# Twelve of 25 blocks of attention weights turned on VectorE and exchanged through DRAM instead of on TensorE

## The chip, the cores and the metric

The kernel runs on one core of a Trainium2 chip. The metric is the device time of one launch in microseconds (us).

## The reference

Attention over 8 batches, 8 heads, 576 positions and 64 channels with a block mask, then a two-layer feed-forward with ELU over 4608 tokens, then a soft mixture of 8 experts with 4 slots each:

```python
scores = scale * np.matmul(q, k.transpose(0, 1, 3, 2))
mask = block_i >= block_j                    # blocks of 64 positions
attn = np.exp(scores - max) / sum            # over the unmasked keys
attn_out = np.matmul(attn, v)
h = x @ w_in                                 # 4608x512 @ 512x2048
g = np.where(h > 0.0, h, np.exp(np.minimum(h, 0.0)) - 1.0)
x = g @ w_out                                # 4608x2048 @ 2048x512
logits = x @ phi                             # 512 x 32 slots
slot_input = softmax(logits, over tokens).T @ x
slot_out = relu(slot_input @ w1) @ w2        # per expert
out = softmax(logits, over slots) @ slot_out
```

All data is float32.

## The kernel before

The work is recorded as operations with an engine, a duration, the buffers read and written and a key (`Plan.add`), and `Plan.order` sets the order by a simulated list schedule: each engine takes, of the operations whose inputs are ready by the planner's durations, the one with the lowest key. On the chip each engine then runs its list in order and waits where an input is late. DMAs are all issued from SyncE's queue (SP), but for the first pair.

**Attention** goes by 32 pairs of heads (four pairs are one batch of 576 tokens). For a pair, `pair_load` and `pair_prep` bring q and k with the channels on partitions. `pair_scores` (four fills, lines 527 to 535) makes the scores on TensorE, takes row maxima on VectorE (L546) and exponentials with row sums on ScalarE (L549); the fourth fill holds the two units (1,0) and (1,1), 128 queries by 256 keys each. `pair_weights` then takes reciprocals (L561, L562), multiplies the weights on GpSimd (L566), and turns them so that the keys lie on partitions: 25 blocks of 128x128 per pair, each one TensorE matmul against the identity (L322), in groups of up to four that go to a PSUM bank and are copied to SBUF by ScalarE or VectorE (L298, L300). A unit (u, h) is 128 queries of head h with 128(u+1) keys, so it has u+1 blocks; the unit "b" holds the last 64 queries of both heads and has five. 8+6+4+2 blocks and those five make 25. `pair_values` multiplies them with v (L632, L636): per pair and head six accumulating pieces of 64, 512, 448, 320, 192 and 64 columns, with the two heads in the two halves of TensorE's columns. The result goes to a ring of two batches (`XR`). The first eight pairs load and scale q and k in another way (`NTP = 8`), and run partly ahead of the rest.

**The feed-forward** goes by 36 tiles of 128 tokens: per tile four ranges of 512 hidden units, per range four steps of three matmuls of 512 columns in fp32r (high and low parts, L669 to L671). Exponential on ScalarE (L674), minimum and maximum on VectorE (L676, L679). In tiles 0 to 29 the hidden units g are turned for the logits without TensorE: VectorE turns 32x32 blocks (`STREAM_TRANSPOSE`, L687), SP writes them to a DRAM tile `turned` (512 KB, twice per tile) and reads them back with the blocks exchanged over partitions (four reads of 128 KB, in runs of 1 KB). `tile_routing` (L711) and `tile_dispatch` (L733 to L771) follow; their 32-column matmuls use a quarter of TensorE's columns each.

**The tail** loads the experts' weights into 23 slots of 1 MB as they come free (among them the attention's SBUF area) and runs the expert layers and the output product.

In idle stretches of the start and of the tail TensorE runs small filler matmuls (L1037). A fp32 matmul shows twice in the trace (two passes) and once in the order of the built program; fp32r matmuls and the identity matmuls show once in both.

The change touches `Plan.add` and `Plan.order` (L77 and L100), `pair_load` (L433), `pair_scores` (L513), `pair_weights` (L552), `pair_values` (L622), the durations handed to the planner in the tile functions, the SBUF area of the turned weights (`PT`), and the key of each pair (`base` in the loop over pairs at the end):

```python
base = T * 4.5 * (b - 1) + 24.0 * p - 24.0 if b else KAS * p + KA0
```

Of the kernel before, what the change touches and what calls it, by code (L numbers as in the profile page):

```python
# [10 lines left out]
F32 = mybir.dt.float32  # L11
# [7 lines left out]
P = 128  # L19
# [5 lines left out]
RING = 2 * S  # L25
KWIN, KWOUT, KWP, KWPS = -92.0, -42.0, 2.0, 2.0
KWS, KWOS, KA0, KAS, KCON, KLD, KSTAGE, NPB = 3.5, 1.0, -109.0, 14.0, -150.0, 30.0, 26.0, 4
NEV, NQ = 16, 1
TLAG, LATE, NTP = 2.5, 30, 8
TICK, DUTY, FILL, FN = 3.4, 0.5, 0.055, 128  # L30
SCALE = 0.125
MASKED = -1e9
# [19 lines left out]
class Plan:  # L52
# [9 lines left out]
    def __init__(self):  # L62
        self.ops = []
        self.writers = {}
        self.readers = {}
        self.fills = []
        self.load = {}
        self.lag = {}

        self.slack = {}  # L70

    def fill(self, dur, fn, after, until):


        self.fills.append((dur, fn, after, until))

    def add(self, engs, dur, fn, r=(), w=(), key=0.0, nbytes=0, load=1.0, lag=1.0, slack=0.0):  # L77
        if isinstance(engs, str):
            engs = (engs,)
        if not isinstance(dur, tuple):  # L80
            dur = (dur,) * len(engs)
        i = len(self.ops)
        deps = set()
        for b in r:
            deps |= set(self.writers.get(b, ()))
        for b in w:
            deps |= set(self.readers.get(b, ()))
            deps |= set(self.writers.get(b, ()))
        for b in r:
            self.readers.setdefault(b, []).append(i)  # L90
        for b in w:
            self.writers[b] = [i]
            self.readers[b] = []
        self.ops.append((engs, dur, fn, deps, key, nbytes))
        self.load[i] = load
        self.lag[i] = lag
        self.slack[i] = slack
        return i

    def order(self):  # L100
        n = len(self.ops)
# [14 lines left out]
        finish = [1e9] * n  # L116
        recent = []
        fillers = {}

        def rested(now):  # L120

# [11 lines left out]
        while events:  # L133
            now = events[0][0]
            while events and events[0][0] <= now + 1e-9:
                _, kind, i = heapq.heappop(events)
                if kind == 0:
                    for e in self.ops[i][0]:
                        heapq.heappush(heaps[e], (self.ops[i][4], i))
            for e in engines:  # L140
                if free[e] > now + 1e-9:
                    continue
                h = heaps[e]
                while h and done[h[0][1]]:
                    heapq.heappop(h)
                if not h:
                    if e == "PE" and rested(now):
                        for d, fn, after, until in self.fills:
                            if finish[after] <= now and not done[until]:
                                seq.append((now, -1, e))  # L150
                                fillers[len(seq) - 1] = fn
                                free[e] = now + d
                                recent.append((now, now + d, 1.0))
                                heapq.heappush(events, (free[e], 1, -1))
                                break
                    continue
                _, i = heapq.heappop(h)
                done[i] = True
                engs, dur, fn, deps, key, nbytes = self.ops[i]
                d = dur[engs.index(e)]  # L160
                busy[e] += d
# [21 lines left out]
        self.span = max(free.values())  # L183
        self.busy = busy
        self.fillers = fillers
        return [(fillers[j] if i < 0 else self.ops[i][2], e) for j, (_, i, e) in enumerate(seq)]


# [16 lines left out]
def attention_moe_kernel(ctx: ExitStack, tc, q, k, v, w_in, w_out, phi, w1, w2, consts, out):  # L205
# [26 lines left out]
    PAD = TT  # L232
    NPT = 2
    PTW = 4 * CHS + S
    PT = aa.take(2 * NPT * PTW)
    RQ = aa.take(2 * S)
    RK = aa.take(2 * S)
    QT = aa.take(2 * S)
# [19 lines left out]
    as_u32 = [t.bitcast(U32) for t in tiles]  # L258
    ps = pp.tile([P, 4096], F32, name="ps")
    wo_f32 = dpool.tile([FF, DM], F32, name="wo_f32")  # L260
    turned = [dpool.tile([P, 1024], F32, name="turned%d" % j) for j in range(2)]
    successors = {}
    marks = {}
# [173 lines left out]
    def pair_load(n, key):  # L437
# [14 lines left out]
        for src, base, nm in ((q, RQ, "rq"), (k, RK, "rk")):  # L452
            for a in range(4):
                h, db = 2 * p + a // 2, a % 2
                load(f(base + S * s, S, 32 * a, 32 * a + 32).rearrange("p (t i) -> p t i", i=32),
                     src[b, h, :, 32 * db:32 * db + 32].rearrange("(t j) i -> j t i", j=32), 340000,
                     w=[(nm, s, a)], key=key, eng=queue(n))

    def pair_load_v(n, key):
# [51 lines left out]
    def pair_scores(n, fill, key):  # L511
# [11 lines left out]
        def sc(e):  # L523
# [15 lines left out]
        add("PE", (0.0 if last else 0.2) + cols / 600, sc, r=([("qb", s, 0), ("qb", s, 1)] if last else [("qt", s)]) + [("kt", s)], w=bkeys, key=key,  # L539
            load=1.0)  # L540
# [13 lines left out]
    def pair_weights(n, half, key):  # L554
# [9 lines left out]
        for x in units:  # L564
            p = pat(x, n)
            add("POOL", (0.28 + wide(x) / 1050) * (1.3 if n < 8 else 1.0), lambda e, x=x, p=p: nc.gpsimd.tensor_scalar(  # L566
                out=f(p, wide(x)), in0=f(p, wide(x)), scalar1=f(rs_col + 9 * s + UNITS[x][0], 1), scalar2=0.0,
                op0=ALU.mult, op1=ALU.add), r=[("rs", s, half)], w=[pkey(x, n)], key=key)

        sl = n % NPT  # L570
        pt = PT + 2 * PTW * sl
# [47 lines left out]

    pt_keys = {}  # L620

    def pair_values(n, key):  # L622
        b, p = divmod(n, 4)
        vs = V + 640 * (n % NV)
        sl = n % NPT
# [12 lines left out]
        add("PE", 2.9, pv, r=rd, w=["ptb", "pvb"], key=key, load=0.25)  # L638
# [22 lines left out]
    def tile_range(i, r, hb, gs, ts, kr):  # L661
# [4 lines left out]
        for kk in range(4):  # L666
# [6 lines left out]
            add("PE", 0.65, hm, r=[("xh", s), ("xl", s), ("wh", r, kk), ("wl", r, kk)], w=[("h", hb)], key=kr)  # L673
# [32 lines left out]
    def tile_routing(kp):  # L706
        def lg(e):
            for c in range(16):
                j = c % 4
                gt = f(GT + 1024 * (c // 8), 1024).rearrange("p (a c j) -> p c a j", a=4, j=32)[:, c % 8]  # L710
                mm(pb(POST, P, 32 * j, 32 * j + 32), lhsT=f(WP + NS * c, NS), rhs=gt, start=(c < 4), stop=(c >= 12))  # L711
        add("PE", 1.0, lg, r=["wp"] + gtk(0) + gtk(1), w=["post"], key=kp, load=0.25)

    def tile_logits(r, ts, bank, bk, kp):
        def lg(e):
            for j in range(4):
                mm(pb(bank, P, 32 * j, 32 * j + 32), lhsT=f(WP + NS * (4 * r + j), NS), rhs=f(ts[0] + P * j, P),
                   start=(r == 0), stop=(r == 3))
        add("PE", 0.3, lg, r=["wp"] + ts[1], w=[bk], key=kp, load=0.25)

    def tile_dispatch(tiles, gs, banks, lps, dtx, dx, kp):

# [46 lines left out]
        add("PE", 0.95 * n, disp, r=[dx[1]] + [gs[t][j][1] for t in range(n) for j in range(4)], w=[bk], key=kp, load=0.25)  # L769
# [35 lines left out]
    def tail(key):  # L805
        att = [(nm, s, a) for nm in ("rq", "rk") for s in range(2) for a in range(4)] + [(nm, s) for nm in ("qt", "kt") for s in range(2)] + \
              [("v", s, j) for s in range(NV) for j in range(3)] + [pkey(x, s) for x in UNITS for s in range(2)] + \
              [x for s in range(NPT) for x in pt_keys[s]]
# [205 lines left out]
    ev = []  # L1014
    for n in range(NPAIR):
        b, p = divmod(n, 4)
        base = T * 4.5 * (b - 1) + 24.0 * p - 24.0 if b else KAS * p + KA0
        ev.append((base - (27 if n < NTP else KLD), lambda n=n, x=base - KLD: pair_load(n, x)))
        ev.append((base - 14, lambda n=n, x=base - 14: pair_prep(n, x)))
        ev.append((base - 16, lambda n=n, x=base - 16: pair_load_v(n, x)))  # L1020
# [4 lines left out]
        ev.append((base + 24, lambda n=n, x=base + 24: pair_values(n, x)))  # L1025
# [46 lines left out]
```

## Time and profile before

| | us |
|---|---|
| three runs, median (lowest to highest) | 993.82 (993.13 to 994.99) |
| profiled execution, span from first to last instruction | 992.1 |
| TensorE busy | 957.2 |
| VectorE, ScalarE, GpSimd busy | 632.8, 474.1, 269.9 |

For the profiled execution the page gives the span; its time outside the span is not told apart, and the span lies 1.7 us below the median of the runs. Engine names in rows: PE is TensorE's matmuls and PEld its weight loads, DVE VectorE, ACT ScalarE, POOL GpSimd, SP SyncE; a q behind the name is the engine's sequencer, as in SPq. L669 is line 669 of the kernel before. Matmuls are pipelined: the duration of one includes its way through the array, so what a matmul costs on the path is read from the chain of waits, which counts each stretch of time once, and not from the mean duration of one.

### The profile page before, as it was taken

How to read it: one execution, taken by the hardware profiler on the slowest of the kernel's cores; microseconds unless marked ns; L12 is line 12 of the kernel's file. 1: busy time of each engine (PE TensorE's matmuls, PEld its weight loads, DVE VectorE, ACT ScalarE, POOL GpSimd, SP SyncE). 2: the span in 40 equal slices, each digit the busy share in tenths (PEclk: the TensorE clock that was granted, in tenths of full speed). 3: DMA queues.
4: the chain of work that ended last, by engine and by line, in shares of the span. 5: the costliest groups of instructions: out<-in, count | busy, mean ns of one | idle time of the engine just before them, and what ended most of it. 6: DMA issues, size and time to landing. Idle time of an engine off the chain costs nothing.

```text
span 992.1 us, 19100 instructions
## 1 busy us (share of the span) xinstructions
PE 957.2 (96%) x6829; PEld 654.1 (66%) x6829; DVE 632.8 (64%) x1612; ACT 474.1 (48%) x1322; POOL 269.9 (27%) x425
## 2 busy tenths in 40 slices
PE   8989999999999999999999999999999999999992
PEld 6657776676666766766666676666666677776351
DVE  5987876566556666667777776777767664444151
ACT  5865555454545555544445444454454343222143
POOL 3852432322212332322332223223232221000000
PEclk9999999999999999999999999999999999999996
DMA  9747567754445445645454445454533249149969
GB/s 239 216 129 214 173 198 177 156 138 127 110 130 142 123 115 126 153 113 141 121 133 123 130 122 137 126 144 115 127 108 101 83 138 401 56 138 326 351 231 354
DMA packets 243998, 160.86 MB, mean 162 GB/s; under 512 B 178624, under 2 KB 209472, under 8 KB 243904
## 3 DMA queue, kind: packets, MB, share of 16 engines
q1 hardware_dynamic: 242704, 159.35, 56.1%
q8 instruction: 54, 0.88, 0.4%
q10 hardware_dynamic: 1200, 0.30, 0.1%
q14 instruction: 40, 0.33, 0.1%
HBM read 114.51 MB, written 45.09 MB: 161 GB/s over the span
## 4 chain that ended last, share of the span: by engine, by line
PE 87%; DMA 4%; ACT 3%; DVE 3%; issue 1%; POOL 1%; SPq 1%; ACTq 0%; DVEq 0%; POOLq 0%
PE ps L669 15%; PE ps L671 13%; PE ps L670 13%; PE ps L322 12%; PE ps L636 8%; PE ps L535 8%; PE ps L767 4%; PE ps L711 3%; PE ps L527 2%; DMA att<-in_moe_w_dram 1%; PE ps L419 1%; DMA g<-in_moe_w_in_dram 1%; PE ps L938 1%; PE ps L1037 1%; ACT att L549 1%; PE ps L733 1%
## 5 line engine op out<-in xcount | busy, mean ns | idle before, releaser
L669 PE MATMUL ps<-w,xhl 128*128 128x512 f32 x576 | 253.3, 440 | 1.2 <-DVE g L679 1.2
L566 POOL TENSOR_SCALAR att<-att,base 128x128 f32<-128x128 f32 (+4 forms) x288 | 177.8, 636 | 206.7 <-DVE base L562 177.7
L671 PE MATMUL ps<-w,xhl 128*128 128x512 f32 x576 | 226.9, 394 | 0.0
L670 PE MATMUL ps<-w,xhl 128*128 128x512 f32 x576 | 226.1, 393 | 0.0
L549 ACT ACTIVATE att<-ps,base 128x128 f32<-128x128 f32 (+4 forms) x288 | 157.8, 553 | 97.1 <-DVE base L546 93.9
L298 ACT COPY att<-ps 128x512 f32<-128x512 f32 (+3 forms) x233 | 110.6, 511 | 92.7 <-PE ps L322 82.4
L546 DVE TENSOR_REDUCE base<-ps 128x1 f32<-128x128 f32 (+4 forms) x288 | 136.5, 502 | 24.4 <-ACT att L549 12.3
L674 ACT ACTIVATE xe<-ps 128x512 f32<-128x512 f32 x144 | 86.2, 599 | 134.7 <-PE ps L671 131.5
L676 DVE TENSOR_SCALAR xe<-xe 128x512 f32<-128x512 f32 x144 | 68.1, 473 | 121.4 <-ACT xe L674 120.9
L669 PEld LDWEIGHTS ps<-w,xhl 128*128 128x128 f32 x576 | 108.3, 188 | 54.7 <-issue 32.7
L322 PE MATMUL ps<-base,att 128*128 128x128 f32 (+1 forms) x880 | 131.1, 279 | 7.4 <-POOL att L566 5.6
L322 PEld LDWEIGHTS ps<-base,att 128*128 128x128 f32 (+1 forms) x880 | 101.4, 142 | 46.0 <-POOL att L566 15.7
L671 PEld LDWEIGHTS ps<-w,xhl 128*128 128x128 f32 x576 | 108.1, 188 | 25.0
L670 PEld LDWEIGHTS ps<-w,xhl 128*128 128x128 f32 x576 | 108.9, 189 | 13.5
L535 PE MATMUL ps<-att 64*128 64x128 f32 (+3 forms) x512 | 96.0, 468 | 3.7 <-ACT att L549 3.6
L679 DVE TENSOR_TENSOR g<-xe,ps 128x512 f32<-128x512 f32 x144 | 97.3, 677 | 2.2
L656 POOL TENSOR_TENSOR xhl<-xe,xhl 128x512 fp32r<-128x512 f32 x36 | 47.3, 1316 | 159.5 <-ACT xhl L654 144.8
L636 PE MATMUL ps<-att 128*64 128x512 f32 (+4 forms) x640 | 88.3, 422 | 0.0
L687 DVE STREAM_TRANSPOSE g<-g 128x512 f32<-128x512 f32 x120 | 82.6, 691 | 3.8 <-DMA turned<-g 1.6
L636 PEld LDWEIGHTS ps<-att 128*64 128x64 f32 x640 | 43.3, 137 | 42.4 <-issue 33.2
L535 PEld LDWEIGHTS ps<-att 64*128 64x128 f32 x512 | 42.0, 185 | 37.9 <-issue 15.7
L487 POOL TENSOR_SCALAR base<-att 64x64 f32<-64x64 f32 x48 | 11.8, 246 | 198.6 <-DVE att L484 141.9
(127 smaller groups left out, 1058.3 us busy)
## 6 DMA issues: line engine op xcount, KB each, us to landing
turned<-g SPq DMA_DIRECT2D x60, 512.0 KB, 3.1
g<-turned SPq DMA_DIRECT2D x240, 128.0 KB, 3.1
att<-in_moe_w_dram SPq DMA_DIRECT2D x11, 1024.0 KB, 13.7
att<-in_v_dram SPq DMA_DIRECT2D x64, 128.0 KB, 3.0
g<-in_moe_w_in_dram SPq DMA_DIRECT2D x16, 512.0 KB, 5.7
w_late<-in_moe_w_dram SPq DMA_DIRECT2D x8, 1024.0 KB, 6.7
out_dram<-att SPq DMA_DIRECT2D x16, 512.0 KB, 5.7
att<-in_q_dram SPq DMA_DIRECT2D x96, 72.0 KB, 2.6
```

Source lines behind the costliest of these rows:

```text
L298: nc.scalar.copy(o, i)
L322: mm(o, lhsT=i, rhs=f(IDN + base, n, base, base + n), start=True, stop=True, is_transpose=True)
L535: mm(pb(at((u, h)), P * (u + 1)), lhsT=f(qt + P * u, P, 64 * h, 64 * h + 64), rhs=f(kt, P * (u + 1), 64 * h, 64 * h + 64), start=True, sto ...
L546: add("DVE", 0.08 + wide(x) / 960, lambda e, x=x, c=c: nc.vector.tensor_reduce(out=f(c, 1), in_=pb(at(x), wide(x)), axis=AX.X, op=ALU.max, ...
L549: add("ACT", 0.50 + wide(x) / 1300, lambda e, x=x, c=c: nc.scalar.activation(f(pat(x, n), wide(x)), pb(at(x), wide(x)), AF.Exp, bias=f(c, ...
L566: add("POOL", (0.28 + wide(x) / 1050) * (1.3 if n < 8 else 1.0), lambda e, x=x, p=p: nc.gpsimd.tensor_scalar(out=f(p, wide(x)), in0=f(p, w ...
L636: mm(pb(PVB + q0 - 64, S - q0, 64 * h, 64 * h + 64), lhsT=f(vs + 320 * h + D * c, D), rhs=f(pts[h] + CHS * c + q0, S - q0), start=(c == 0) ...
L669: mm(pb(bank, 512), lhsT=fr(xh + P * kk, P), rhs=hi, start=(kk == 0), stop=False)
L670: mm(pb(bank, 512), lhsT=fr(xh + P * kk, P), rhs=lo, start=False, stop=False)
L671: mm(pb(bank, 512), lhsT=fr(xl + P * kk, P), rhs=hi, start=False, stop=(kk == 3))
L674: add("ACT", 0.48, lambda e: nc.scalar.activation(f(ee, 512), pb(bank, 512), AF.Exp), r=[("h", hb)], w=[("e", hb)], key=kr)
L679: add("DVE", 0.6, lambda e: nc.vector.tensor_tensor(out=f(g, 512), in0=f(ee, 512), in1=pb(bank, 512), op=ALU.max), r=[("e", hb), ("h", hb) ...
```

## The change

From pair 9 on (`n >= NTP`, 24 pairs) the 12 blocks that lie in the first 256 keys of the units (3,h), (2,h) and (1,h) are no longer turned on TensorE. VectorE turns their 32x32 blocks (six instructions of 256 columns per pair) into `TU`. SP writes the 768 KB to a DRAM tile `swapped` and reads them back into `PX` with four DMAs of 192 KB, in runs of 1536 bytes, one for each quarter of the partitions. The other 13 blocks stay on TensorE, in groups of 4, 4, 4 and 1, and go to `PY`. The product with v has eight pieces per head now: 128 columns for itself, then 384 and 64 for each of the first two key blocks, then 320, 192 and 64; the two pieces of 384 columns read `PX` in runs of 32 elements. The key of those pairs is 8 lower (`EARLY`). The planner's durations of several operations change, a change of TensorE's tiling (full, row halves, column halves, column quarters) is charged 0.13, and of operations with the same key TensorE's list takes one of the current tiling first.

```diff
+EARLY = 8.0
+CHANGE, STAY, JOIN = 0.13, 0.0, 0.0
...
+                if e == "PE":
+                    if self.mode[i] != tiling:
+                        d += CHANGE
...
-    PT = aa.take(2 * NPT * PTW)
+    XW, YW = 12 * 32, 3 * P + 320 + 192
+    PT = aa.take(max(2 * NPT * PTW, 16 * XW + 4 * YW))
+    TU, PX, PY = PT, PT + 8 * XW, PT + 16 * XW
...
+    swapped = [dpool.tile([P, 4 * XW], F32, name="swapped%d" % j) for j in range(2)]
...
-                     src[b, h, :, 32 * db:32 * db + 32].rearrange("(t j) i -> j t i", j=32), 340000,
+                     src[b, h, :, 32 * db:32 * db + 32].rearrange("(t j) i -> j t i", j=32), 180000,
...
+        if n >= NTP:
+            pair_swap(n, half, key)
+            return
...
+        for x in HALVES[half]:
+            if x == "b" or x[0] == 0:
+                continue
+            o = f(tu, 4 * XW).rearrange("p (m h c u j) -> p h u c m j", m=4, h=2, c=2, j=32)[:, x[1], x[0] - 1]
+            add("DVE", 0.1 + 256 / 960, lambda e, x=x, o=o: nc.vector.transpose(
+                out=o, in_=f(pat(x, n), 256).rearrange("p (c m i) -> p c m i", c=2, m=4)),
+                r=[pkey(x, n)], w=[("tu", sl, x)], key=key)
...
+        groups = (
+            [("b", c) for c in range(4)],
+            [((3, h), c) for h in range(2) for c in (2, 3)],
+        ) if half == 0 else (
+            [((2, 0), 2), ((2, 1), 2), ((0, 0), 0), ((0, 1), 0)],
+            [("b", 4)],
+        )
...
+        via = swapped[sl]
+        load(via, f(tu, 4 * XW), 4 * P * 4 * XW, r=[("tu", sl, x) for x in UNITS], w=[("pvia", sl)], key=key, lag=TLAG)
+        for m in range(4):
+            load(f(px, 4 * XW, 32 * m, 32 * m + 32).rearrange("i (a y) -> i a y", a=4),
+                 via.rearrange("(a i) (m y) -> m i a y", a=4, m=4)[m], 4 * 32 * 4 * XW, r=[("pvia", sl)], w=[("px", sl, m)], key=key, lag=TLAG)
...
+            go(PTB, P, 0, lambda h: both[:, h, 0:P], True, True)
+            for c in range(2):
+                go(PVB, 384, c, lambda h: px[:, h, c], c == 0, False)
+                go(PVB + 384, 64, c, lambda h: both[:, h, P + 64 * c:P + 64 * c + 64], False, False)
+            for c in range(2, 5):
+                w = S - P * c
+                go(PVB + 448 - w, w, c, lambda h: both[:, h, NEAR[c]:NEAR[c] + w], False, c == 4)
...
-        base = T * 4.5 * (b - 1) + 24.0 * p - 24.0 if b else KAS * p + KA0
+        base = T * 4.5 * (b - 1) + 24.0 * p - 24.0 - (EARLY if n >= NTP else 0.0) if b else KAS * p + KA0
```

How the order moves, first TensorE in the middle of the program, the stretch up to the product with v of one pair. Before (L322 turns blocks, L535 is scores, L767 the dispatch, L632 and L636 the product with v):

```order
L322 MATMUL ps<-base,att 128x128 x7
L669 MATMUL ps<-w_71,xhl 128x512
L670 MATMUL ps<-w_71,xhl 128x512
L671 MATMUL ps<-w_71,xhl 128x512
...
L322 MATMUL ps<-base,att 128x128 x6
...
L632 MATMUL ps<-att 64x64 x2
L636 MATMUL ps<-att 64x512 x2
L636 MATMUL ps<-att 64x448 x2
L636 MATMUL ps<-att 64x320 x2
L636 MATMUL ps<-att 64x192 x2
L636 MATMUL ps<-att 64x64 x2
```

The same stretch of the change (L359 turns blocks, L795 to L797 are the three passes, L734 the product with v, L572 scores):

```order
L359 MATMUL ps<-base,att 128x128 x4
...
L359 MATMUL ps<-base,att 128x128
L734 MATMUL ps<-att 64x128 x2
L734 MATMUL ps<-att 64x384 x2
L734 MATMUL ps<-att 64x64 x2
L734 MATMUL ps<-att 64x384 x2
L734 MATMUL ps<-att 64x64 x2
L734 MATMUL ps<-att 64x320 x2
L734 MATMUL ps<-att 64x192 x2
L734 MATMUL ps<-att 64x64 x2
L572 MATMUL ps<-att 128x256 x2
```

The groups that turn blocks have shrunk, and the product with v has eight pieces in place of six; the scores of 256 columns that stand behind it belong to the next pair.

Then SP's queue, where the first exchanged pair comes up (turned and swapped are the DRAM tiles). Before:

```order
L317 DMA att<-in_k_dram 32x18x32 x4
L317 DMA g<-turned_75 32x4x256 x4
L317 DMA turned_74<-g 128x1024
L317 DMA att<-in_v_dram 128x4x64 x2
L317 DMA att<-in_v_dram 64x2x64
L317 DMA g<-turned_74 32x4x256 x4
```

The change:

```order
L354 DMA att<-in_k_dram 32x18x32 x4
L354 DMA swapped_74<-att 128x1536
L354 DMA g<-turned_77 32x4x256 x4
L354 DMA turned_76<-g 128x1024
L354 DMA att<-swapped_74 32x4x384 x4
L354 DMA g<-turned_76 32x4x256 x4
L354 DMA att<-in_v_dram 128x4x64 x2
```

The write of `swapped` and its four reads stand among the loads and the exchanges of the tiles, and a write of `turned` stands between them.

## Rows read from the trace of the kernel before

**Rows 1.** The page: busy time and share of the span by engine.

```profile
PE 957.2 (96%) x6829; PEld 654.1 (66%) x6829; DVE 632.8 (64%) x1612; ACT 474.1 (48%) x1322; POOL 269.9 (27%) x425
```

**Rows 2.** Windows: length, busy by engine (instructions), granted clock, DMA share, GB/s.

```profile
200.00:816.00 616.00, 614.76 (x4170) 423.09 (x4168) 422.10 (x1114) 297.41 (x871) 178.64 (x306) 1.00 0.47 124
...
500.00:600.00 100.00, 100.00 (x672) 69.38 (x673) 72.62 (x193) 47.37 (x141) 29.61 (x52) 1.00 0.50 130
...
900.00:950.00 50.00, 48.25 (x465) 24.31 (x467) 14.47 (x33) 11.17 (x24) 0.00 (x0) 1.00 0.98 355
```

**Rows 3.** Waits of PE: who waited for whom, total us, times, longest.

```profile
PE ps L322 <- POOL att L566: 5.6, 9, 1.1
PE ps L535 <- ACT att L549: 3.6, 3, 2.2
...
PE ps L938 <- DMA att<-in_moe_w_dram: 0.3, 1, 0.3
```

**Rows 4.** Chain of waits, 400 to 440 us: start, us on the chain, what.

```profile
402.21 0.76 PE ps L322 x7
...
404.36 0.66 PE ps L322 x6
...
406.40 0.27 PE ps L632 x4
406.67 2.59 PE ps L636 x20
409.26 1.06 PE ps L535 x4
410.32 0.43 PE ps L669
410.75 0.23 PE ps L670
...
413.94 1.07 PE ps L535 x8
...
415.90 1.01 PE ps L711 x32
416.91 1.02 PE ps L322 x8
...
419.08 0.44 PE ps L322 x4
...
421.72 1.00 PE ps L767 x8
422.72 0.63 PE ps L535 x4
...
427.68 0.97 PE ps L527 x4
```

**Rows 5.** Chain of waits in the last tiles: logits from turned g in plain columns.

```profile
827.35 0.57 PE ps L717 x16
...
885.45 0.36 PE ps L717 x8
```

**Rows 6.** Timeline of POOL: the six multiplications of one pair's second half.

```profile
427.47 2.93 POOL L566 TENSOR_SCALAR att<-att,base 128x384 f32<-128x384 f32 x6
```

**Rows 7.** The page: VectorE's turning of g.

```profile
L687 DVE STREAM_TRANSPOSE g<-g 128x512 f32<-128x512 f32 x120 | 82.6, 691 | 3.8 <-DMA turned<-g 1.6
```

**Rows 8.** DMA issues: what, count, KB each, median us from issue to landing.

```profile
turned<-g SPq DMA_DIRECT2D x60, 512.0 KB, 3.1
g<-turned SPq DMA_DIRECT2D x240, 128.0 KB, 3.1
```

**Rows 9.** DMAs of turned, 200 to 300 us: time to landing.

```profile
DMA to landing us min/median/max: 2.6/3.0/5.4
```

**Rows 10.** Timeline of SP: start, us until the last is issued, what.

```profile
445.09 1.74 SPq L317 DMA_DIRECT2D g<-turned  x4
```

**Rows 11.** Waits of SP's queue from 800 to 910 us.

```profile
SPq L838 <- POOL xhl L656: 43.1, 2, 42.4
```

More of the change, by code (lines that the diff above doesn't have):

```diff
@@ L70, in __init__, with add @@
         self.slack = {}
+        self.mode = {}
     def fill(self, dur, fn, after, until):
         self.fills.append((dur, fn, after, until))
-    def add(self, engs, dur, fn, r=(), w=(), key=0.0, nbytes=0, load=1.0, lag=1.0, slack=0.0):
+    def add(self, engs, dur, fn, r=(), w=(), key=0.0, nbytes=0, load=1.0, lag=1.0, slack=0.0, mode="F"):
         if isinstance(engs, str):
@@ L97, in add, with pick @@
         self.slack[i] = slack
+        self.mode[i] = mode
         return i
+    def pick(self, heap, done, mode):
+        while heap and done[heap[0][1]]:
+            heapq.heappop(heap)
+        if not heap:
+            return None
+        top = heap[0]
+        if self.mode[top[1]] != mode:
+            far = top[0] + (STAY if mode == "F" else JOIN)
+            best = None
+            for key, i in heap:
+                if done[i] or key > far:
+                    continue
+                m = self.mode[i]
+                if m == mode or mode != "F" and m != "F":
+                    rank = (m != mode, key, i)
+                    if best is None or rank < best:
+                        best = rank
+            if best is not None:
+                return best[2]
+        return top[1]
     def order(self):
@@ L118, in order @@
         fillers = {}
+        tiling, changes = "F", 0
         def rested(now):
@@ L145, in order @@
                     heapq.heappop(h)
+                chosen = self.pick(h, done, tiling) if e == "PE" else None
                 if not h:
@@ L156, in order @@
                     continue
-                _, i = heapq.heappop(h)
+                i = heapq.heappop(h)[1] if chosen is None else chosen
                 done[i] = True
@@ L160, in order @@
                 d = dur[engs.index(e)]
+                if e == "PE":
+                    if self.mode[i] != tiling:
+                        d += CHANGE
+                        changes += 1
+                    tiling = self.mode[i]
                 busy[e] += d
@@ L185, in order @@
         self.fillers = fillers
+        self.changes = changes
         return [(fillers[j] if i < 0 else self.ops[i][2], e) for j, (_, i, e) in enumerate(seq)]
@@ L538, in pair_scores @@
         last = fill == 0 and n >= NTP
-        add("PE", (0.0 if last else 0.2) + cols / 600, sc, r=([("qb", s, 0), ("qb", s, 1)] if last else [("qt", s)]) + [("kt", s)], w=bkeys, key=key,
-            load=1.0)
+        add("PE", (0.0 if last else 0.15) + cols / 600, sc, r=([("qb", s, 0), ("qb", s, 1)] if last else [("qt", s)]) + [("kt", s)], w=bkeys, key=key,
+            load=1.0, mode="F" if last else "R")
         for x in units:
@@ new lines, in swapped_values, with pv, go @@
+    def swapped_values(n, key):
+        b, p = divmod(n, 4)
+        sl = n % 2
+        vs = V + 640 * (n % NV)
+        px = f(PX + 4 * XW * sl, 4 * XW).rearrange("p (a h c u j) -> p h c u a j", a=4, h=2, c=2, j=32)
+        both = f(PY + 2 * YW * sl, 2 * YW).rearrange("p (h w) -> p h w", h=2)
+        ring = XR + RING * p + S * (b % 2)
+        def pv(e):
+            def go(o, w, c, rhs, start, stop):
+                for h in range(2):
+                    mm(pb(o, w, 64 * h, 64 * h + 64), lhsT=f(vs + 320 * h + D * c, D), rhs=rhs(h), start=start, stop=stop)
+            go(PTB, P, 0, lambda h: both[:, h, 0:P], True, True)
+            for c in range(2):
+                go(PVB, 384, c, lambda h: px[:, h, c], c == 0, False)
[3 more added lines that the diff above has]
+                go(PVB + 448 - w, w, c, lambda h: both[:, h, NEAR[c]:NEAR[c] + w], False, c == 4)
+        add("PE", 3.0, pv, r=[("v", n % NV, j) for j in range(3)] + swap_keys(sl), w=["ptb", "pvb"], key=key, load=0.25, mode="C")
+        add(*evict(n, P), lambda e: copy(e, f(ring, P), pb(PTB, P)), r=["ptb"], w=[("xr", p, b % 2, 0)], key=key)
+        add(*evict(n, 448), lambda e: copy(e, f(ring + P, 448), pb(PVB, 448)), r=["pvb"], w=[("xr", p, b % 2, 1)], key=key)
@@ L622, in pair_values @@
     def pair_values(n, key):
+        if n >= NTP:
+            return swapped_values(n, key)
         b, p = divmod(n, 4)
@@ L672, in tile_range @@
             marks["hm"] = len(plan.ops)
-            add("PE", 0.65, hm, r=[("xh", s), ("xl", s), ("wh", r, kk), ("wl", r, kk)], w=[("h", hb)], key=kr)
+            add("PE", 0.7, hm, r=[("xh", s), ("xl", s), ("wh", r, kk), ("wl", r, kk)], w=[("h", hb)], key=kr)
         add("ACT", 0.48, lambda e: nc.scalar.activation(f(ee, 512), pb(bank, 512), AF.Exp),
@@ L711, in lg @@
                 mm(pb(POST, P, 32 * j, 32 * j + 32), lhsT=f(WP + NS * c, NS), rhs=gt, start=(c < 4), stop=(c >= 12))
-        add("PE", 1.0, lg, r=["wp"] + gtk(0) + gtk(1), w=["post"], key=kp, load=0.25)
+        add("PE", 0.9, lg, mode="D", r=["wp"] + gtk(0) + gtk(1), w=["post"], key=kp, load=0.25)
     def tile_logits(r, ts, bank, bk, kp):
@@ L718, in lg @@
                    start=(r == 0), stop=(r == 3))
-        add("PE", 0.3, lg, r=["wp"] + ts[1], w=[bk], key=kp, load=0.25)
+        add("PE", 0.25, lg, mode="D", r=["wp"] + ts[1], w=[bk], key=kp, load=0.25)
     def tile_dispatch(tiles, gs, banks, lps, dtx, dx, kp):
@@ L768, in disp @@
                        start=(t == 0), stop=(t == n - 1))
-        add("PE", 0.95 * n, disp, r=[dx[1]] + [gs[t][j][1] for t in range(n) for j in range(4)], w=[bk], key=kp, load=0.25)
+        add("PE", 0.88 * n, disp, mode="D", r=[dx[1]] + [gs[t][j][1] for t in range(n) for j in range(4)], w=[bk], key=kp, load=0.25)
         for x in range(0, 512, 512 // n):
@@ L807, in tail @@
               [("v", s, j) for s in range(NV) for j in range(3)] + [pkey(x, s) for x in UNITS for s in range(2)] + \
-              [x for s in range(NPT) for x in pt_keys[s]]
+              [x for s in range(NPT) for x in pt_keys[s]] + [("tu", s, x) for s in range(2) for x in UNITS] + swap_keys(0) + swap_keys(1)
         gk = [("g", s) for s in range(NG)]
@@ L1024, in attention_moe_kernel @@
             ev.append((base + 9 * h + 7, lambda n=n, h=h, x=base + 9 * h + 7: pair_weights(n, h, x)))
-        ev.append((base + 24, lambda n=n, x=base + 24: pair_values(n, x)))
+        ev.append((max(base + 24, T * 4.5 * (b - 1) + 0.1 if n >= NTP else -1e9), lambda n=n, x=base + 24: pair_values(n, x)))
     for i in range(NTILE - 2):
```

37 lines of the change are left out of this document (36 added, 1 removed).

## The prediction

> **What bounds the kernel now.** I read the page's busy times first: TensorE is busy 96% of the span, no other engine above 66% [rows 1]. A share over the whole span can hide a stage with another limit, so the windows come next: from 200 to 816 us, where nearly all of the 24 changed pairs run, TensorE is busy 614.76 of 616 us at a granted clock of 1.00, the DMA engines are busy 0.47 of the time, and VectorE, ACT and POOL have room [rows 2]. A busy TensorE could still be held by small waits, so I looked at its waits: over the whole run the largest sum is 5.6 us, and all that it waited for a DMA is 0.3 us [rows 3]. In this stretch, then, the time is the sum of TensorE's work, and the chain of waits, which counts each moment once, gives what each piece of that work costs [rows 4].
>
> **Turned blocks.** In the chain 4, 6 and 7 turned blocks take 0.44, 0.66 and 0.76 us [rows 4]: 0.11 each, with nothing fixed per group. (The 1.02 for 8 stands behind the column-quartered logits and holds the price of that change of tiling, 1.02 less 8 times 0.11, that is 0.14.) The change takes away 12 blocks in 24 pairs, 288: **31.7 us less**. Nothing on TensorE hides them, as it does not wait.
>
> Here a rule speaks against the change. The chain has TensorE at 0.11 a block [rows 4], VectorE turns 512 columns (four blocks) in 0.691 us, 0.17 a block [rows 7], and TensorE is the one that is full. The Trainium skill, page "VectorE: DVE Perf Modes", section "Rules for kernel authors", says to turn a 128x128 block on TensorE if PSUM may be the destination, and to use VectorE for 32x32; by it this term would be a loss and not a gain. The rows side with the rule on the price of one block and not on which engine has the time.
>
> **Product with v.** The columns per pair and head stay 1600. The old product takes 0.27 for its first piece of 64 and 2.59 for the other five with 1536 columns [rows 4]. New are two more pieces per pair, 48 in all. The scores give the price of a column of such a pair of heads: 1.06 for 512 and 0.63 for 256 [rows 4] are 1.68 ns each. 1536 columns at that are 2.58 us, which leaves 0.01 for the starts of all five pieces. The other bound is the first piece, 0.27 against 0.11 for 64 columns, 0.16, though that holds the change of tiling. Bounds: 0.3 to 7.7 us. I take 0.04 each, nearer to the inner pieces, since both new ones are inside a row of pieces: **1.9 us more**. Reading `PX` in runs of 32 elements I cost at nothing: the logits of the turned tiles read runs of 32 too, and take 1.01 for 16 matmuls, while the ones from plain columns take 0.57 for 8 and 0.36 for 4 [rows 4, 5]; per matmul past the start that is 0.055 either way.
>
> **Changes of tiling.** In the order of the built programs TensorE changes its tiling 413 times before and 402 times now. In the chain a step behind scores costs 0.43 against 0.23 (0.20), the one behind the column quarters 0.14 [rows 4]. 11 fewer at 0.17: **1.9 us less**.
>
> **Copies, VectorE, ACT.** The copies from PSUM fall from 3200 to 1664 columns a pair; six turnings of 256 columns come, half of 0.691 each, 2.1 us a pair [rows 7]. Four pairs fall in some 97 us, so VectorE, at 72.6 of 100 in its fullest window [rows 2], rises by 9 at most and less as copies go. It has no place on the path unless it passes 100. Cost nothing.
>
> **DMA.** Each changed pair moves 768 KB out and back, 1.57 MB, so 6.3 MB in 100 us. Where the DMA engines were full they moved 355 GB/s at a share of 0.98 [rows 2]; 6.3 MB are 18 us of that, and the share goes from 0.50 to some 0.68. Cost nothing by itself.
>
> **The new wait.** The product with v of a pair now waits for a trip: fourth scores, exponentials, sums, six multiplications on POOL, VectorE, write, four reads. TensorE takes its list in order, so if the trip is late all matmuls queue behind. From the rows: the fourth scores start at 422.72 and POOL is done with that pair at 427.47 + 2.93 = 430.40 [rows 4, 6], 7.7 us. The last turning with one other VectorE operation ahead, 1.0 [rows 7]. Issue of the write, a quarter of 1.74, 0.4 [rows 10]; its landing, 3.1 for 512 KB [rows 8] and 0.7 for 256 KB more at 355 GB/s [rows 2], 3.8. Four issues 1.7 [rows 10], the landing of the last 3.1 [rows 8] and 0.2 for 64 KB more, 3.3. Sum **17.9 us**. What stands on TensorE between the fourth scores of a pair and its product with v, by the order of the changed program, is 54 matmuls of the three passes in a usual pair (42 to 60): 54 at 0.23 is 12.4, and with 13 blocks at 0.11, the scores 0.63, 0.97, 1.06 and 1.07, one logits 1.01, one dispatch 1.00 [rows 4] and three starts behind scores at 0.20 some **20 us** (before it was 21 to 33 such matmuls). So the shift of the key by 8 just covers the trip: 2 us to spare in a usual pair, none in the two with 42. SP's queue is passed too: the reads stand behind a write of `turned` that waits for VectorE, and the write of `swapped` holds back the reads of a tile's g, which have waited for nothing on TensorE so far [rows 3]. I take **3 us more** in all, with 0 as one bound; the other is the rivals' matter.
>
> **Ends.** The start keeps its operations and nearly its order of DMAs. At the end 240 matmuls of the three passes stand behind the last product with v, 249 before, so the attention's SBUF is given back some 2 us later relative to the end. What hides that: SP's queue stood 42.4 us in one wait for POOL's use of `xhl` while loading the experts' weights [rows 11]. Without that cover it would be 2 us. Cost nothing.
>
> **Sum.** 31.7 less, 1.9 more, 1.9 less, 3 more: 28.7 less. Against the profiled span of 992.1 that is 963.4; the median of the runs lies 1.7 above the span, so **965.0 us**.
>
> **Rivals.**
> 1. *The trip is a little late in most pairs.* For it: a spare of 2 us against landings of turned's DMAs that reach 5.4 where 3.0 is usual [rows 9], and more traffic on the same engines. Against: the exchanges of g ran without a wait on TensorE [rows 3]. At 0.5 to 1.2 us for each of 24 pairs it adds 12 to 29 us to a sum of 31.7 less: 976 to 993, of which the part above 980 is this case, say 985.
> 2. *Slower: the trip costs more than the blocks.* The place is TensorE's wait ahead of the product with v; it decides from 31.7 / 24 = 1.3 us a pair. If write and reads both landed at 5.4 and not near 3 [rows 9], the trip would be 17.9 + 2.3 + 2.3 = 22.5, 2.5 over the 20, and 24 pairs would pay 60 against 31.7 gained, some 1022; at 1.7 over, 1003. I say 1010. Against: 5.4 is the largest of its window, not the usual one. The page "VectorE: DVE Perf Modes" of the Trainium skill, section "The three transpose paths", warns that a plain DMA that turns by strides is 19 times slower than the one through the crossbar if the innermost stride is large. Turned's reads, which have contiguous runs of 1 KB, land in 3.1 us [rows 8], and the new runs are longer.
> 3. *No gain.* TensorE's turned blocks were only filling time that something else sets, as the exchange of g on VectorE and SP, which now has more behind it: 992 to 996. Against: no wait on TensorE in this stretch [rows 2, 3].
>
> **How the numbers follow.** My forecast's own range takes the bounds of the pieces (0.3 to 7.7), no stall to 10 us of it, and a block at up to 1.02 / 8 = 0.128 [rows 4]: 956 to 980. It has 0.82, rival 1 above 980 has 0.08, rival 2 has 0.05, rival 3 has 0.05. The range 956 to 980 leaves out 0.18. Faster by over 0.2% (about what a measurement of this kernel can tell from no change, 2 us): 0.90; within: 0.05; slower: 0.05.
>
> **What would show it.** Right: TensorE's group of turned attention blocks loses 288 instructions and some 32 us; from 200 to 800 us TensorE stays above 98% busy at a clock of 1.00; a product with v takes 2.9 to 3.0 us in the chain; waits of the first piece of the product for DMA `swapped` sum to a few us; a DMA share near 0.68. Wrong: a large sum in the row of that wait (rivals 1 and 2), a product of 3.1 us or more (the pieces mis-sized), waits of the logits' matmuls for g (SP's queue), or the same span of the stretch with an idle TensorE (rival 3).

## The result, and the profile after

The changed kernel takes 967.62 us in the median (966.97 to 969.34), the kernel before 994.40 in the same runs; the ratio is 0.9736 [0.9721, 0.9751], 26.8 us less. The forecast was 965.0 in a range of 956 to 980.

The page of the changed kernel, busy time by engine (against [rows 1]), at a span of 964.9 us:

```profile
PE 924.7 (96%) x6708; PEld 628.0 (65%) x6708; DVE 666.2 (69%) x1739; ACT 453.1 (47%) x1336; POOL 275.4 (29%) x428
```

TensorE's busy time fell by 32.5 us and the span by 27.2, so 5.3 us came up in which it stands. The group of turned attention blocks, before and after, accounts for the fall (busy time, then the mean of one):

```profile
L322 PE MATMUL ps<-base,att 128*128 128x128 f32 x864 | 127.2, 279 | 6.8 <-POOL att L566 5.6 <-ACT att L298 0.8
```

```profile
L359 PE MATMUL ps<-base,att 128*128 128x128 f32 x576 | 94.5, 282 | 10.1 <-POOL att L603 8.6 <-ACT att L335 1.3
```

Windows of the changed kernel, columns as in [rows 2]:

```profile
200.00:800.00 600.00, 594.82 (x4200) 406.66 (x4199) 461.58 (x1267) 281.14 (x906) 186.17 (x311) 1.00 0.77 195
...
500.00:600.00 100.00, 99.58 (x704) 67.88 (x702) 80.05 (x224) 47.06 (x152) 30.55 (x52) 1.00 0.83 199
```

TensorE stood 1.2 us from 200 to 816 before, and stands 5.2 from 200 to 800 now, at the same granted clock of 1.00. VectorE went from 72.6 to 80 in the window from 500 to 600 and the DMA engines from 0.50 to 0.83; over the long stretch the DMA share went from 0.47 to 0.77. Who TensorE waited for, 200 to 800 us:

```profile
PE ps L359 <- DVE g L805: 1.4, 1, 1.4
PE ps L359 <- ACT base L868: 0.9, 1, 0.9
PE ps L797 <- POOL xhl L782: 0.9, 2, 0.6
PE ps L359 <- ACT att L335: 0.8, 1, 0.8
PE ps L859 <- DVE base L855: 0.4, 1, 0.4
PE ps L734 <- DMA att<-swapped: 0.4, 1, 0.4
```

The new wait, the product with v (L734) for the exchanged blocks, is the last of six rows; the other stops have no common cause in this list. The chain of waits from 400 to 440 us gives the prices (against [rows 4]; L734 is the product, L359 turned blocks):

```profile
403.61 2.89 PE ps L734 x32
...
413.91 0.44 PE ps L359 x4
...
427.15 2.87 PE ps L734 x32
```

A block still costs 0.11. The product with its eight pieces costs 2.87 to 2.89, against 0.27 + 2.59 = 2.86. The page's row for VectorE's new instruction, and its DMA issues:

```profile
L678 DVE STREAM_TRANSPOSE att<-att 128x256 f32<-128x256 f32 x144 | 57.5, 417 | 2.8 <-POOL att L603 2.7
```

```profile
swapped<-att SPq DMA_DIRECT2D x24, 768.0 KB, 4.2
att<-swapped SPq DMA_DIRECT2D x96, 192.0 KB, 4.3
```

And one trip in SP's timeline; the pair's fourth scores start at 406.40 and its product with v at 427.15:

```profile
415.13 0.35 SPq L354 DMA_DIRECT2D swapped<-att  x1
418.47 0.35 SPq L354 DMA_DIRECT2D turned<-g  x1
418.92 2.51 SPq L354 DMA_DIRECT2D att<-swapped  x4
```

By the landings in the trace the last read, issued at 421.0, is in at 425.9: 19.5 us after the scores, 1.2 before the product starts. Over all 24 pairs the trip takes 17.1 to 22.7 us with a median of 19.7; the product starts 20.8 us behind the fourth scores in the median, and 0.8 is left between the two. (The first of its pieces, 128 columns, doesn't read the exchanged blocks.)

### The profile page after: what moved, and what is told of

Same layout as the page of the kernel before. It is cut to its first block, busy times and chain, and to the rows that moved or that the text cites. A ratio compares the mean times of both kernels' runs of the same rounds, so it can differ in the third digit from the quotient of the medians.

```text
span 964.9 us, 19123 instructions
## 1 busy us (share of the span) xinstructions
PE 924.7 (96%) x6708; PEld 628.0 (65%) x6708; DVE 666.2 (69%) x1739; ACT 453.1 (47%) x1336; POOL 275.4 (29%) x428
## 4 chain that ended last, share of the span: by engine, by line
PE 80%; DMA 6%; DVE 6%; POOL 2%; issue 2%; ACT 2%; SPq 1%; ACTq 0%; POOLq 0%; DVEq 0%
PE ps L795 14%; PE ps L797 13%; PE ps L796 12%; PE ps L359 8%; PE ps L572 7%; PE ps L734 7%; PE ps L893 3%; PE ps L837 3%; PE ps L564 2%; POOL att L603 2%; DVE g L427 1%; DMA g<-in_moe_w_out_dram 1%; DMA att<-in_moe_w_dram 1%; PE ps L1163 1%; PE ps L456 1%
## 5 line engine op out<-in xcount | busy, mean ns | idle before, releaser
L603 POOL TENSOR_SCALAR att<-att,base 128x128 f32<-128x128 f32 (+4 forms) x288 | 185.0, 660 | 260.8 <-DVE base L599 165.0
L795 PE MATMUL ps<-w,xhl 128*128 128x512 f32 x576 | 253.1, 439 | 0.0
L797 PE MATMUL ps<-w,xhl 128*128 128x512 f32 x576 | 227.2, 394 | 0.9 <-POOL xhl L782 0.9
L795 PEld LDWEIGHTS ps<-w,xhl 128*128 128x128 f32 x576 | 109.1, 189 | 48.5 <-issue 27.0
L335 ACT COPY att<-ps 128x256 f32<-128x256 f32 (+3 forms) x241 | 86.0, 409 | 109.6 <-PE ps L359 105.7
L797 PEld LDWEIGHTS ps<-w,xhl 128*128 128x128 f32 x576 | 108.1, 188 | 26.5 <-POOL xhl L782 1.8
L359 PE MATMUL ps<-base,att 128*128 128x128 f32 x592 | 98.4, 281 | 10.7 <-POOL att L603 8.6
L359 PEld LDWEIGHTS ps<-base,att 128*128 128x128 f32 x592 | 69.0, 142 | 45.8 <-issue 16.6
L572 PE MATMUL ps<-att 64*128 64x128 f32 (+3 forms) x512 | 95.9, 468 | 1.2 <-ACT att L586 1.2
L734 PE MATMUL ps<-att 128*64 128x64 f32 (+4 forms) x768 | 71.4, 337 | 0.5 <-DMA att<-swapped 0.4
L572 PEld LDWEIGHTS ps<-att 64*128 64x128 f32 x512 | 41.8, 185 | 37.7 <-issue 17.3
L734 PEld LDWEIGHTS ps<-att 128*64 128x64 f32 x768 | 43.8, 137 | 32.2 <-issue 22.7
L678 DVE STREAM_TRANSPOSE att<-att 128x256 f32<-128x256 f32 x144 | 57.5, 417 | 2.8 <-POOL att L603 2.7
```

The costliest lines, as they stand in the source:

```text
L335: nc.scalar.copy(o, i)
L359: mm(o, lhsT=i, rhs=f(IDN + base, n, base, base + n), start=True, stop=True, is_transpose=True)
L572: mm(pb(at((u, h)), P * (u + 1)), lhsT=f(qt + P * u, P, 64 * h, 64 * h + 64), rhs=f(kt, P * (u + 1), 64 * h, 64 * h + 64), start=True, sto ...
L734: mm(pb(o, w, 64 * h, 64 * h + 64), lhsT=f(vs + 320 * h + D * c, D), rhs=rhs(h), start=start, stop=stop)
L795: mm(pb(bank, 512), lhsT=fr(xh + P * kk, P), rhs=hi, start=(kk == 0), stop=False)
```

## The experiments

Theory: the time is TensorE's work, the 288 blocks are the gain, and the trip is just covered. The rivals were the planner's new rules as the cause of the gain, and DMA or VectorE as the cause of the new stops. "Before" beside each is the kernel before on the same chip, 994.0 to 995.2 us, and the ratio is to that. "Slower than the changed kernel" is by the medians, against the 967.62 us above, which was not measured again beside the experiments; by the ratios such a difference comes out up to 2.4 us less or 1 us more.

### The planner alone, and the exchange alone

e1 keeps all blocks on TensorE and takes the new planner:

```diff
+SW = 99
...
-        if n >= NTP:
+        if n >= SW:
             pair_swap(n, half, key)
```

> The changed planner (its durations, the charge for a change of tiling, the choice by tiling) without the exchange: all 25 blocks of every pair stay on TensorE and the keys are not shifted. TensorE changes tiling 409 times against 413. Theory (the gain is the work of the 288 blocks on TensorE): 4 fewer changes at 0.17 are 0.7 us, so 992 to 995 beside some 994 for the kernel before. Rival (a good part of the 27 us comes from the better order): 970 to 988.

993.83 us, ratio 0.9982 [0.9964, 0.9999]: 1.8 us less by the ratio, 0.9 by the medians. The new order by itself is worth next to nothing; the rival falls.

e2 has the exchange and the shift, with the planner's old numbers and without its choice by tiling (its main lines):

```diff
-CHANGE, STAY, JOIN = 0.13, 0.0, 0.0
+CHANGE, STAY, JOIN = 0.0, 0.0, 0.0
...
-                chosen = self.pick(h, done, tiling) if e == "PE" else None
+                chosen = self.pick(h, done, tiling) if False else None
...
-                     src[b, h, :, 32 * db:32 * db + 32].rearrange("(t j) i -> j t i", j=32), 180000,
+                     src[b, h, :, 32 * db:32 * db + 32].rearrange("(t j) i -> j t i", j=32), 340000,
...
-            add("PE", 0.7, hm, r=[("xh", s), ("xl", s), ("wh", r, kk), ("wl", r, kk)], w=[("h", hb)], key=kr)
+            add("PE", 0.65, hm, r=[("xh", s), ("xl", s), ("wh", r, kk), ("wl", r, kk)], w=[("h", hb)], key=kr)
```

> The exchange with the key shift, but the planner's durations, DMA sizes and choice as in the kernel before. Changes of tiling 408 against 402. Theory: the blocks are gone from TensorE all the same, so 966 to 972, a little over the changed kernel's 967.6 by 6 changes of tiling (1 us) and by waits where the old durations place things worse. Rival (the new durations are what keeps the trip covered): over 975, with waits for the exchanged blocks of 10 us or more in TensorE's list of waits.

985.78 us, ratio 0.9909 [0.9881, 0.9938]: 9 us gained in place of 27. The theory missed; the rival's time is right, but not its reason, as the waits for exchanged blocks are 1.2 us. Two windows of e2:

```profile
600.00:610.00 10.00, 6.17 (x38) 2.76 (x33) 7.51 (x26) 4.13 (x14) 2.31 (x3) 0.97 0.75 218
610.00:620.00 10.00, 7.50 (x37) 4.26 (x38) 3.86 (x12) 2.70 (x12) 3.85 (x9) 0.52 1.04 181
```

SP's and TensorE's timelines there:

```profile
600.46 0.44 SPq L354 DMA_DIRECT2D swapped<-att  x1
601.33 2.53 SPq L354 DMA_DIRECT2D g<-turned  x4
607.54 0.34 SPq L354 DMA_DIRECT2D turned<-g  x1
607.98 2.21 SPq L354 DMA_DIRECT2D att<-swapped  x4
```

```profile
603.64 0.33 PE L359 MATMUL ps<-base 128*128 128x128 f32 x1 [1.14 <-ACT base L868]
...
611.33 1.57 PE L572 MATMUL ps<-att 64*128 64x256 f32 x4 [2.44 <-ACT att L586]
612.83 0.69 PE L734 MATMUL ps<-att 128*64 128x128 f32 x4
614.69 5.12 PE L734 MATMUL ps<-att 128*64 128x384 f32 x28 [1.17 <-DMA att<-swapped]
```

The reads of one pair stand behind a write of `turned` that SP could issue only at 607.5, 7.1 us after the write they belong to. But most of TensorE's stops there are not for them: up to 611.33 it waits for ScalarE, with small waits for VectorE and GpSimd (in brackets the wait before a row: 1.14 and 2.44 are the largest), and for the exchanged blocks only 1.17 us at 614.69. TensorE is busy 6.17 of 10 us, next its granted clock is 0.52, nearly all at 1.2 GHz. The four scores matmuls at 611.33, ahead of the wait for the exchanged blocks, already take 1.57 us where they take 0.70 in the changed kernel, and the pieces of the product with v take 5.8 us where they take 2.9. From 200 to 800 us e2 stands 14.1 us against 5.2, and the clock is 0.95 and 0.98 in two windows of 100 us. So the exchange with the shift alone brings a third of the gain; the rest needs lists that fit.

e9 takes away only the charge for a change of tiling and the choice by it:

```diff
-CHANGE, STAY, JOIN = 0.13, 0.0, 0.0
+CHANGE, STAY, JOIN = 0.0, 0.0, 0.0
...
-                chosen = self.pick(h, done, tiling) if e == "PE" else None
+                chosen = self.pick(h, done, tiling) if False else None
```

> The changed kernel with its new durations, but without the charge of 0.13 for a change of tiling and without the choice by tiling: one part of what the swap with the old planner lacked. Theory (the planner's clock must run like the chip's so that SP's and VectorE's lists fit TensorE's; the charge is some 400 times 0.13, 52 us in 900, so without it everything but TensorE is planned too early): 972 to 988. Rival (the durations of the matmuls are what matters, the charge is not): 966 to 971.

976.72 us, ratio 0.9807 [0.9783, 0.9831]: 9 us of e2's 18 go with the charge and the choice (by the ratios 7 of 17), with the changes of tiling all but the same (one more than the changed kernel's 402). So fewer changes are not what counts. That it is the planner's clock is argued: the charge and the choice were not taken apart. Which of the other numbers makes the other 9 was not tried.

### How many pairs

e3 exchanges from pair 21 on, e8 from pair 5 on (with PSUM bank `PTB` alone for pairs 5 to 8, as before):

```diff
-        if n >= NTP:
+        if n >= SW:          # 20 in e3, 4 in e8
             pair_swap(n, half, key)
```

> The exchange only from pair 21 on, 12 pairs in place of 24, 144 blocks. Theory (0.11 us a block, nothing fixed): half of the 26.8 us, so 979 to 983. Rival (a gain or loss that is there once, from planner or ends): away from the middle, under 975 or over 987.

982.72 us, ratio 0.9868 [0.9843, 0.9894]: for half of the pairs 12.0 us less by the medians and 13.1 by the ratio, where all of them bring 26.8 and 26.3. Half within the noise, as the theory has it.

> The exchange from pair 5 on, four pairs more, 48 blocks. These pairs run between 84 and 200 us, where TensorE is busy 97 to 98% and DMA engines 0.7 of the time. Theory: TensorE's work bounds there too, 48 blocks at 0.11 are 5.3 us: 962 to 964. Rival (in that stretch the exchange meets loads and POOL is slower, so the trip is late or other waits come up): 966 to 972, with waits ahead of the product with v.

973.42 us, ratio 0.9770 [0.9747, 0.9794]: 48 more blocks gone, and 5.8 us slower than the changed kernel by the medians, 3.4 by the ratios, whose intervals just touch. The gain of 5.3 us did not come and the theory missed. The rival has the direction, with a time 1.4 us above its range. A window of e8 (the profile is of its slowest execution), and the waits of TensorE from 84 to 260 us:

```profile
160.00:180.00 20.00, 13.33 (x67) 8.29 (x65) 11.59 (x31) 8.22 (x23) 6.09 (x12) 0.80 0.94 196
```

```profile
PE ps L573 <- ACT att L587: 6.6, 3, 3.3
PE ps L735 <- DMA att<-swapped: 2.3, 1, 2.3
```

From 84 to 200 us the DMA share is 0.85 against 0.74 in the changed kernel, TensorE is busy 105.7 us against 114.0, and its clock is 0.94: waits, and a clock that falls behind them, cost more than the blocks give. The larger wait is that of the scores (L573) for ScalarE's exponentials; ahead of the product (L735) it is 2.3 us.

### The spare of the trip

e5 tells the planner that the exchange lands at once:

```diff
-        load(via, f(tu, 4 * XW), 4 * P * 4 * XW, r=[("tu", sl, x) for x in UNITS], w=[("pvia", sl)], key=key, lag=TLAG)
+        load(via, f(tu, 4 * XW), 4 * P * 4 * XW, r=[("tu", sl, x) for x in UNITS], w=[("pvia", sl)], key=key, lag=0.0)
...
-                 via.rearrange("(a i) (m y) -> m i a y", a=4, m=4)[m], 4 * 32 * 4 * XW, r=[("pvia", sl)], w=[("px", sl, m)], key=key, lag=TLAG)
+                 via.rearrange("(a i) (m y) -> m i a y", a=4, m=4)[m], 4 * 32 * 4 * XW, r=[("pvia", sl)], w=[("px", sl, m)], key=key, lag=0.0)
```

> The planner is told that the exchange's write and reads land with no lag behind their transfer (0 for 2.5 each), so it puts the product with v earlier: between the fourth scores and it stand 46 matmuls of the three passes on average in place of 54, some 1.8 us less. Theory (the trip takes 18 to 19 us and has 1 to 2 us to spare in the changed kernel): the wait for the exchanged blocks goes from 0.4 us to 8 to 30 us in sum, 973 to 995. Rival (the trip lands with 4 us and more to spare): the wait stays under 3 us, 965 to 970.

1027.38 us, ratio 1.0318 [1.0293, 1.0343], 60 us over the changed kernel and 32 over the kernel before. TensorE's wait, the window, and the page's busy times at a span of 1024.9:

```profile
PE ps L734 <- DMA att<-swapped: 41.9, 19, 3.6
```

```profile
200.00:800.00 600.00, 557.21 (x3800) 379.72 (x3798) 428.13 (x1181) 257.99 (x831) 175.31 (x293) 0.98 0.69 177
```

```profile
PE 942.5 (92%) x6708; PEld 638.7 (62%) x6708; DVE 667.2 (65%) x1753; ACT 448.7 (44%) x1322; POOL 277.9 (27%) x428
```

By the planner the product comes 1.8 us earlier on average; on the chip its start lies 17.3 us behind the fourth scores in the median of 24 pairs, where it was 20.8, while the trip is as long as before (19.4 against 19.7). So 19 pairs now wait 2.2 us each: in the usual pair hardly anything was spare. Of the 60 us, 42 are stops of TensorE (82.4 us over the span against 40.2), and 18 are its same 6708 matmuls taking longer, 942.5 us against 924.7. The mean clock over the span fell from 0.991 to 0.975. Some of that is not the trips': the first 84 us, ahead of any exchanged pair, show 0.96 against 1.00, by estimate 3 us (0.04 of 84), where the 0.98 from 200 to 800 is 12 (0.02 of 600). Both theories put the time too low; the direction is the theory's.

e4 takes the shift of the keys away (`EARLY = 0.0`):

> The changed kernel without the shift of the pairs' keys by 8. The planner still puts each product with v behind its trip; what the shift moves is how much other work TensorE has ready meanwhile, above all for the last pair of a batch (33 to 42 matmuls between its fourth scores and its product). Theory (the shift is what covers the trip of a batch's last pair): idle of 10 to 25 us from 200 to 800 us, 972 to 990. Rival (the planner's order covers the trip by itself, the shift is not needed): 965 to 971.

984.50 us, ratio 0.9916 [0.9887, 0.9946], 17 us slower than the changed kernel, the time and the idle time that the theory has; its profile is of the slowest execution, span 990.4:

```profile
200.00:800.00 600.00, 586.09 (x4044) 395.60 (x4043) 452.94 (x1239) 275.07 (x892) 179.58 (x305) 0.99 0.74 187
```

TensorE stands 13.9 us in place of 5.2, and the waits for `swapped` are only 2.3 of it. The shift is needed, but not for the product's wait alone; that it is the last pair of a batch which needs it is not shown.

e4b doubles the shift (`EARLY = 16.0`). With that the first exchanged pair is recorded ahead of pair 8's product and overwrites its turned weights, so one product computes with other numbers; the work is the same.

> The shift of the keys doubled to 16. Theory (8 covers the trip, more only makes pairs ready earlier): 965 to 971. Rival (earlier pairs hold buffers longer and bunch the exchanges, so the queue and VectorE are hit in bursts): 972 to 985.

974.37 us, ratio 0.9799 [0.9777, 0.9821], 7 us slower than at 8: the rival's side in time; its reason was not looked for. 8 is better than 0 and than 16.

### Who causes the new stops

e6 does each turning on VectorE twice, e7 adds a write of 768 KB per pair that nobody reads:

```diff
+            for _ in range(2):
+                add("DVE", 0.1 + 256 / 960, lambda e, x=x, o=o: nc.vector.transpose(
...
```

> Each of VectorE's 144 turnings of attention blocks is done twice, and the planner knows it. VectorE gets some 58 us more work. Theory (the 5 us that TensorE stands idle from 200 to 800 us in the changed kernel come from VectorE being fuller, 77% there): idle of 10 to 25 us there, 972 to 987. Rival (they come from the fuller DMA engines and SP's queue): 966 to 971.

1002.14 us, ratio 1.0059 [1.0042, 1.0077], 35 us slower than the changed kernel, and 0.6% slower than before. The turnings take 50.6 us more (108.1 against 57.5); VectorE's busy time is 35 us more (701.2 against 666.2), as some of its copies went to ScalarE (23 operations more there). The window, and rows of TensorE's waits in it:

```profile
200.00:800.00 600.00, 577.59 (x3964) 392.67 (x3964) 480.04 (x1337) 275.64 (x891) 176.69 (x301) 0.98 0.74 183
```

```profile
PE ps L838 <- DMA g<-turned: 6.0, 3, 2.8
PE ps L796 <- DVE g L806: 4.7, 3, 2.0
...
PE ps L735 <- DMA att<-swapped: 0.3, 1, 0.3
```

VectorE is busy 80% there and not 100, yet TensorE stands 22.4 us. The two largest rows are waits for the feed-forward's g, from its exchange and from VectorE; for the exchanged blocks it waits next to nothing. The idle time is as the theory has it; the time is 15 us above its range, with a mean clock of 0.973 in place of 0.991.

```diff
+        load(spare[sl], f(tu, 4 * XW), 4 * P * 4 * XW, r=[("tu", sl, x) for x in UNITS], w=[("spare", sl)], key=key, lag=TLAG)
```

> Behind the four reads of each pair SP issues one more write of the 768 KB, to a DRAM tile that nobody reads: 18.9 MB more, DMA share from 0.77 to some 0.86 between 200 and 800 us. Theory (VectorE, not DMA, is behind the idle): 966 to 971. Rival (DMA and SP's queue are behind it): TensorE waits more for turned or swapped, 972 to 987.

989.17 us, ratio 0.9937 [0.9915, 0.9960], 22 us slower than the changed kernel. TensorE's wait in e7 and the landings of DMAs of `swapped`:

```profile
PE ps L736 <- DMA att<-swapped: 8.5, 10, 1.5
```

```profile
DMA to landing us min/median/max: 2.9/5.1/10.4
```

The time is above the rival's range too. The theory (VectorE, not DMA) fell: either addition costs time, and far more than the stops it was to explain. e7 puts both bytes on the engines and an entry in SP's queue, and doesn't tell these two apart.

e10 sends all attention copies to ScalarE (`NEV = 99`):

> All copies of attention blocks and results out of PSUM go to ScalarE (47% busy from 200 to 800 us), some 40 fewer on VectorE (77%). Theory (VectorE has next to nothing to spare, so relief shows): idle from 200 to 800 us falls from 5 to 1 to 3 us, 962 to 966. Rival (ScalarE's list is in the chain too, its exponentials come later): 968 to 976.

971.59 us, ratio 0.9774 [0.9747, 0.9802]. VectorE's busy time from 200 to 800 fell from 461.6 to 441.9 us, and TensorE stands 6.9 us there, not less. Missed; the time is in the rival's range. 20 us less on VectorE, given to ScalarE, do not take the last 5 us of stops away.

e11 multiplies the units without exchanged blocks last:

```diff
-        for x in units:
+        for x in sorted(units, key=lambda x: n >= NTP and x != "b" and x[0] == 0):
             p = pat(x, n)
```

> POOL multiplies the units (0,h), which have no exchanged block, last in the second half, so the last exchanged unit is ready two short multiplications (0.7 us) earlier; the planner knows. Theory (the trip has no spare to speak of, and the planner turns the 0.7 us into an earlier product with v, not into spare): within 3 us of the changed kernel, 964 to 971. Rival (a shorter trip frees TensorE's list): 960 to 964.

967.33 us, ratio 0.9727 [0.9703, 0.9751]: the same as the changed kernel, with 3.9 us of stops from 200 to 800. No version tried is faster by more than a measurement can tell.

## Why the prediction was right, and where it was not

**Turned blocks, 31.7 less.** Right. TensorE's group of turned attention blocks lost 288 instructions and 32.7 us (127.2 to 94.5), e3 shows the gain halved with half of the pairs. No run leaves the blocks out without an exchange, so their price is read from the group and the chain. The rule of the Trainium skill, page "VectorE: DVE Perf Modes", section "Rules for kernel authors" (a 128x128 block on TensorE where PSUM may be the destination), would have kept them where they were; the measurement decides against it in this kernel, where TensorE is the engine that is full.

**Product with v, 1.9 more.** Mis-sized: 2.88 against 2.86, 0.5 us in 24 pairs, near the lower bound. (That bound is 0.3 in the text; 0.01 us for five starts makes it 0.1 for 48.) At 0.01 us per new piece, starts inside a row of pieces and runs of 32 elements cost next to nothing here.

**Changes of tiling, 1.9 less.** Not separated. e1, with 4 changes fewer and nothing else removed, gained 0.9 to 1.8 us with an interval that nearly reaches 0.

**The new wait, 3 more.** The size is near, the place is not. The wait itself is 0.4 us. The other stops bring what TensorE's idle time has grown by to 5.3 us over the span, and rows of VectorE, ScalarE and POOL stand in its list. The trip I put at 17.9 takes 19.7 in the median. By its pieces, scores to the write's issue 8.7 (7.7 + 1.0) and the write to the first read 4.3 (0.4 + 3.8) were right; the step that was mis-sized is the landing of the last read, 4.8 us and not 3.3. What TensorE has in between, 20.8, was near the 20. So the spare was not 2 us but 0.8, which e5 bears out.

**VectorE and DMA at nothing.** Here the step "It has no place on the path unless it passes 100" failed, though the time came out. VectorE at 80% and the DMA engines at 0.77 to 0.83 (I had 0.68: the exchange took 30 to 33 us of the engines in 100, from 0.47 to 0.77 and from 0.50 to 0.83, not 18) have no room left in the sense that counts: e6 and e7 add to them and lose 35 and 22 us. That what I took for cover is a schedule that fits closely is my reading of e2, e5, e6 and e7 together. The changed planner numbers, which I priced at 11 changes of tiling, make it fit: without them 18 of the 27 us are gone (e2).

**Ends.** Right: from 879 us to the end the last 86 us hold 65.81 us of TensorE's work, the same as the last 86 before.

**The sum.** That it came within 3 us is in part luck: the product was priced 1.4 us too high and the stops 2.3 too low, and nothing in the sum stood for how closely the lists must fit. Two bounds don't follow from their terms: 12 to 29 us on a sum of 31.7 less make 974 to 991 for rival 1, not 976 to 993, and the bounds of the pieces make some 955 to 978 for the range; neither changes the answer.

Rival 2 is what e5 and e6 became: a late trip, or a late VectorE, costs more than the blocks bring. Its mechanism is real, and the forecast held because the changed kernel stands just on the right side (0.8 us a pair). What makes the remaining 5 us of stops is open: relief of VectorE (e10) and POOL's order for a shorter trip (e11) did not remove them.

## What to carry to other kernels

Where the chain of waits shows one engine full, price what leaves it by the chain and not by an instruction's mean duration; here 288 times 0.11 us came out to within 1 us of the group's busy time. Work moved to an engine at 70% was free here only while the order still fitted: ask of each list in turn, SP's queue too, what stands behind a late entry. When lists are written from planned durations, the planner's durations belong to the change, and a shortfall of 2 us per trip (e5) cost its length and then the clock.

## What the runs showed of the hardware that was not expected

After TensorE had been busy 6.2 of 10 us, its granted clock was 0.52 in the next 10 us (e2), and the 32 instructions of a product took 5.8 us in place of 2.9. In e5, with waits for the exchanged blocks of at most 3.6 us each, the granted clock from 200 to 800 us was 0.98 where the changed kernel has 1.00, and the same matmuls took 18 us more of TensorE's time over the span, in which the first 84 us, ahead of the exchange, had 0.96 as well. VectorE's turning of 256 columns takes 417 ns and of 512 columns 691 [rows 7]: half the columns cost six tenths.
